# Attention and two MLPs on one core: the last block of the first MLP issued in another order, its weight splits and narrowings cut in two

## The chip, the cores and the metric

One core of a Trainium2 chip runs the whole program in one launch. The metric is the device time of one execution in microseconds (us); lower is better. A time of a kernel is the median of several executions, and the profile shows one execution of its own.

## The reference

Windowed attention with a few global keys, then two MLPs over 1536 tokens of width 512, all in float32:

```
x  = softmax(scale * q k^T + bias, masked) v      # 2 x 8 heads x 768 x 64, as 1536 x 512
h  = x @ w_in;  x = (h * cos(h)) @ w_out          # first MLP, hidden width 2048
g  = x @ w_gate; v = x @ w_val                    # second MLP, hidden width 1536
out = (g * sigmoid(g) * v) @ w_out2
```

To keep float32 accuracy, each operand of a matrix product is split into a rounded high part and a remainder, and three products are summed: high x high, high x remainder, remainder x high.

## The kernel before, in words

The tokens are three blocks of 512 (`BLOCKS`). The first MLP runs 16 hidden slices of 128 for each block, so 48 steps; a step is written s, and the last block is s = 32 to 47. The attention of the later tokens is woven into steps 0 to 31. The second MLP then runs 12 slices for each of the three blocks (`run`).

A step of the first MLP has these parts:

- `h_mm(s)`: 12 matmuls on TensorE (L278) that write one of two PSUM banks `h`. In each group of three the third is the first that needs the remainder of the weight.
- `chain_a(s)` on ScalarE (L304: rounded k = h / 2pi), `chain_f(s)` on VectorE (L315: the fraction f), `chain_sin(s)` on ScalarE (L324 sine, L325 square), then `chain_c(s)`: L331 on VectorE (the product with h), L335 on ScalarE (the high part of g), L336 (the remainder of g) on VectorE or GpSimd.
- `prep_in(s)` and `prep_out(s)` split a weight tile: a cast on ScalarE (L217, high part) and a subtraction (L218, remainder) on VectorE or GpSimd, in the last block always on VectorE. Each kind has two buffers.
- `y_mm(s)`: 12 matmuls (L349) that add slice s into four PSUM banks `y`; three matmuls for each bank, of which the third needs the remainder of the weight. It is issued two steps late: `y_mm(s-2)` follows `h_mm(s)`. At the end of a block the four banks are evicted by ScalarE (L358) and VectorE (L359), and the next block's first `y` product needs them free.

The weights come as 8-byte words. `fetch` starts a DMA into one of three staging tiles `st` (L193, queue of SyncE), and `narrow` makes float32 of them with three VectorE operations (L198, L201, L204). During the last block of the first MLP the weights of the second MLP are fetched and narrowed ahead: `ahead(u, half)`, with u = s - 32, calls `conv()`, which narrows one tile and starts the next DMA. In `run` two more are narrowed in each step, and any that is missing when a split needs it.

Up to step 31 the planner of the compiler orders each engine's instructions. `last_block()` opens a region (`manual_schedule`) in which each engine issues in exactly the order in which the code emits; engines wait for one another only through data and buffers. All that the change reorders lies in this region. Its loop before is L402 to L411:

```python
        for s in range(last, nsteps):
            chain_a(s, h_mm(s))
            prep_in(s + 1)
            chain_f(s)
            prep_out(s - 1)
            chain_sin(s)
            ahead(s - last, 0)
            chain_c(s)
            ahead(s - last, 1)
            y_mm(s - 2)
```

Of the kernel before, what the change touches and what calls it, by code (L numbers as in the profile page):

```python
# [15 lines left out]
I32 = mybir.dt.int32  # L16
AF = mybir.ActivationFunctionType
ALU = mybir.AluOpType
# [4 lines left out]
P = 128  # L23
B, H, S, D = 2, 8, 768, 64
NTOK = B * S
DM = H * D
# [44 lines left out]
LD = 5  # L71
BASES = (0, 3, 6, 8, 13, 17, 20, 23)
HN = 256
AHEAD2 = (4, 8, 12)
BLOCKS = ((0, 512), (512, 512), (1024, 512))


# [1 line left out]
def attention_moe_moe2_kernel(  # L79
# [14 lines left out]
    nc = tc.nc  # L94
    NF1 = w1i.shape[0]
# [3 lines left out]
    def f32(ap):  # L99
        return ap.bitcast(F32)  # L100
# [4 lines left out]
    ws_p = ctx.enter_context(tc.tile_pool(name="ws", bufs=2))  # L105
# [17 lines left out]
    def load_q(i):  # L123
# [16 lines left out]
        out=nval, in0=nneg, scalar=4294967296.0, in1=nf[:, :, 0], op0=ALU.mult, op1=ALU.add  # L140
# [45 lines left out]
    def fetch(src, j, pool=wr_p, tag="w"):  # L186

        if not wide:
            w = pool.tile([P, DM], F32, tag=tag, name="w")
            nc.sync.dma_start(out=w, in_=src[j])  # L190
            return lambda: w
        t = st_p.tile([P, DM, 2], I32, tag="st", name="st")
        nc.sync.dma_start(out=t, in_=src[j].bitcast(I32).rearrange("p (n w) -> p n w", w=2))  # L193

        def narrow():
            w = pool.tile([P, DM], I32, tag=tag, name="w")
            hi, lo = t[:, :, 1], t[:, :, 0]
            nc.vector.tensor_scalar(  # L198
                w, hi, 0x07FFFFFF, 3, op0=ALU.bitwise_and, op1=ALU.logical_shift_left
            )  # L200
            nc.vector.scalar_tensor_tensor(  # L201
                out=w, in0=hi, scalar=-(1 << 30), in1=w, op0=ALU.bitwise_and, op1=ALU.bitwise_or
            )
            nc.vector.scalar_tensor_tensor(  # L204
                out=w, in0=lo, scalar=29, in1=w,
                op0=ALU.logical_shift_right, op1=ALU.bitwise_or,
            )
            return w.bitcast(F32)

        return narrow  # L210

    def eng(which, n):
        return nc.vector if n < len(which) and which[n] == "D" else nc.gpsimd

    def split_w(w, tag, e=nc.gpsimd, pool=ws_p):
        s = pool.tile([P, 2, DM], F32R, tag=tag, name="ws")
        nc.scalar.copy(out=s[:, 0, :], in_=w)  # L217
        e.tensor_tensor(out=s[:, 1, :], in0=w, in1=f32(s[:, 0, :]), op=ALU.subtract)  # L218
        return s

    def x_turn(xn, ps_pool, tag):
# [12 lines left out]
    def moe(before, steps, release):  # L234

        with ExitStack() as c1:
            got = []

            def last_block(*pools):
                release()
                c1.enter_context(tc.manual_schedule())
                got.append(second_mlp(c1, *pools))
                return got[0][0]

            rest = first_mlp(c1, before, steps, last_block)
            got[0][1](rest)

    def first_mlp(c1, before, steps, last_block):  # L250
        w_in, w_out = {}, {}
        got = {}
        todo = [(b, j) for b in range(len(BLOCKS)) for j in range(NF1)]
        nsteps = len(todo)
        hp = c1.enter_context(tc.tile_pool(name="hp", bufs=2, space=PSUM))
        wis, wos, hps, hs, fs, gs, ys = {}, {}, {}, {}, {}, {}, {}
# [34 lines left out]
        def h_mm(s):  # L291
            n = BLOCKS[todo[s][0]][1]
            if s in hps:
                h_part(s, HN, n)
            else:
                hps[s] = hp.tile([P, 512], F32, tag="h", name="h")
                h_part(s, 0, n)
            wis.pop(s)
            return hps.pop(s)

        def chain_a(s, ps):
            n = BLOCKS[todo[s][0]][1]
# [23 lines left out]

        def chain_c(s):
            n = BLOCKS[todo[s][0]][1]
            h, f = hs.pop(s)[0], fs.pop(s)
            g = g_p.tile([P, 2, 512], F32R, tag="g", name="g")  # L330
            nc.vector.scalar_tensor_tensor(  # L331
                out=f[:, :n], in0=f[:, :n], scalar=0.5, in1=h[:, :n],
                op0=ALU.subtract, op1=ALU.mult,
            )
            nc.scalar.copy(out=g[:, 0, :n], in_=f[:, :n])  # L335
            eng(GLE, s).tensor_tensor(  # L336
                out=g[:, 1, :n], in0=f[:, :n], in1=f32(g[:, 0, :n]), op=ALU.subtract
            )
            gs[s] = g

        def y_mm(s):
            b, j = todo[s]
# [30 lines left out]
        ch_p = c1.enter_context(tc.tile_pool(name="ch", bufs=2))  # L373
        g_p = c1.enter_context(tc.tile_pool(name="g", bufs=2))
        yp = c1.enter_context(tc.tile_pool(name="yp", bufs=4, space=PSUM))
        last = nsteps - NF1
        for s in range(last):
            early, late = steps.get(s, ((), ()))
            if s < NF1:
                get("i", s + 2)  # L380
                get("o", s + 1)
            ps = h_mm(s)
            if s >= 2:
                y_mm(s - 2)
            prep_in(s + 1)
            if s >= 1:
                chain_b(s - 1)
            for th in early:
                th()
            if s >= 1:  # L390
                chain_c(s - 1)
            if s < NF1:
                use("i", w_in, s + 2)
                use("o", w_out, s)
            prep_out(s - 1)
            chain_a(s, ps)
            for th in late:
                th()
        ahead = last_block(ch_p, g_p, hp, yp)
        chain_b(last - 1)  # L400
        chain_c(last - 1)
        for s in range(last, nsteps):  # L402
            chain_a(s, h_mm(s))
            prep_in(s + 1)
            chain_f(s)
            prep_out(s - 1)
            chain_sin(s)
            ahead(s - last, 0)
            chain_c(s)
            ahead(s - last, 1)  # L410
            y_mm(s - 2)  # L411
        prep_out(nsteps - 1)
        return [lambda s=s: y_mm(s) for s in (nsteps - 2, nsteps - 1)]

    def second_mlp(c2, ch_p, g_p, hp, yp):


        todo = [(b, j) for b in range(len(BLOCKS)) for j in range(NF2)]
        nsteps = len(todo)
# [23 lines left out]
        def prep(nm, s):  # L443
            if s < nsteps:
                pool, tag = split_pool[nm]
                while (nm, todo[s][1]) not in w2:
                    conv()
                wsp[nm, s] = split_w(w2[nm, todo[s][1]], tag, nc.vector, pool)
# [59 lines left out]
                    nc.sync.dma_start(out=out[rows, :], in_=o)  # L508

        def ahead(u, half):  # L510
            if u == 0 and half == 0:
                get()
                get()
            if u > 0 and (half == 1 or u in AHEAD2):
                conv()
            if u == NF1 - 1 and half == 1:
                prep("g", 0)
                prep("v", 0)

        def run(rest):  # L520
            for s in range(nsteps + 1):
# [15 lines left out]
                    for _ in range(2):  # L537
                        conv()

        return ahead, run  # L540

    def windowed_path():
        m1 = const.tile([P, 3, P], F32, name="m1")
# [545 lines left out]
```

## Time and profile before

| | |
|---|---|
| time, median of 3 executions | 748.09 us (745.61 to 751.55) |
| the profiled execution | 748.84 us, span 747.0 us |
| TensorE busy | 692.3 us, 93% of the span |
| VectorE busy | 491.6 us, 66% |
| ScalarE busy | 380.0 us, 51% |
| GpSimd busy | 156.8 us, 21% |
| mean granted TensorE clock | 0.943 of full |

The span is the time from the first to the last instruction that the profile records; 1.84 us of the profiled execution lie outside it. Busy shares are means over stages that differ: the last block of the first MLP and the change to the second MLP lie between about 322 and 447 us, and only that stretch is read closely below.

### The profile page before, as it was taken

The page shows a single profiled execution, that of the slowest core. Times are in us where ns is not written, and L with a number is a line of the kernel's source. Part 1 is how long each engine was busy: PE and PEld are TensorE (multiplying, and loading weights), DVE is VectorE, ACT ScalarE, POOL GpSimd, SP SyncE. Part 2 cuts the span into 40 slices and gives each one's busy share as a digit, 9 for nine tenths or more (in the row PEclk, how much of TensorE's full clock was granted, in tenths as well). Part 3 has the DMA queues.
Part 4 walks back from the last instruction along what each step waited for, and adds up shares of the span by engine and source line. Part 5 has one row for each costly group of instructions (what it writes and reads, how often), then busy time and mean ns, then how long its engine had stood idle before and what let it go on. Part 6 is the DMA issues. An engine that isn't in the chain of part 4 may idle for free.

```text
span 747.0 us, 9145 instructions
## 1 busy us (share of the span) xinstructions
PE 692.3 (93%) x3280; PEld 532.5 (71%) x3282; DVE 491.6 (66%) x950; ACT 380.0 (51%) x770; POOL 156.8 (21%) x135
## 2 busy tenths in 40 slices
PE   8897797998999999998888789999999999999996
PEld 3355575766677778876666568888888888888884
DVE  5778999999986675438778748977344434343441
ACT  2664657566498889655544543333343333333331
POOL 2545553654545535420000000000000000000000
PEclk8856898799999999999999979999999999999999
DMA  6769746755541232002332313440010000100001
GB/s 211 163 151 229 211 129 185 172 134 171 147 123 43 57 61 41 17 1 60 110 112 85 95 46 113 141 142 28 1 57 0 1 0 1 57 0 1 1 0 61
DMA packets 69510, 62.73 MB, mean 84 GB/s; under 512 B 48881, under 2 KB 55025, under 8 KB 69457
## 3 DMA queue, kind: packets, MB, share of 16 engines
q1 hardware_dynamic: 69456, 62.08, 30.6%
q8 instruction: 27, 0.44, 0.2%
q14 instruction: 27, 0.21, 0.1%
HBM read 47.19 MB, written 3.15 MB: 67 GB/s over the span
## 4 chain that ended last, share of the span: by engine, by line
PE 64%; DVE 25%; ACT 5%; DMA 3%; issue 2%; DVEq 0%; SPq 0%; ACTq 0%
PE v L458 13%; PE g L458 13%; PE o L494 13%; PE h L278 8%; PE y L349 7%; PE s L696 6%; DVE w L201 4%; DVE w L204 4%; DVE w L198 3%; DVE f L331 2%; DVE f L315 2%; DVE ws L218 2%; DMA st<-w1i 2%; DVE g L336 2%; DVE sb L715 1%
## 5 line engine op out<-in xcount | busy, mean ns | idle before, releaser
L218 DVE TENSOR_TENSOR ws<-w,ws 128x512 fp32r<-128x512 f32 x160 | 113.1, 729 | 108.3 <-ACT ws L217 108.2
L278 PE MATMUL h<-xh,ws 128*128 128x512 f32 (+1 forms) x392 | 138.6, 415 | 17.5 <-DVE ws L218 10.1
L349 PE MATMUL y<-g,ws 128*128 128x512 f32 x576 | 141.5, 394 | 4.1 <-DVE xl L359 3.0
L349 PEld LDWEIGHTS y<-g,ws 128*128 128x128 f32 x576 | 109.0, 190 | 29.2 <-DVE xl L359 3.4
L217 ACT CAST ws<-w 128x512 fp32r<-128x512 f32 x204 | 120.2, 615 | 9.8 <-PE y L349 3.6
L278 PEld LDWEIGHTS h<-xh,ws 128*128 128x128 f32 x392 | 76.1, 199 | 44.5 <-DVE ws L218 15.5
L494 PE MATMUL o<-ws,a 128*128 128x512 f32 x432 | 104.9, 392 | 0.0
L458 PE MATMUL g<-xh,ws 128*128 128x512 f32 x288 | 96.9, 398 | 5.8 <-ACT ws L217 4.5
L458 PE MATMUL v<-xh,ws 128*128 128x512 f32 x288 | 96.3, 395 | 0.0
L494 PEld LDWEIGHTS o<-ws,a 128*128 128x128 f32 x432 | 81.0, 188 | 18.7 <-DVE a L481 0.4
L278 PE MATMUL h<-xl,ws 128*128 128x512 f32 (+1 forms) x196 | 79.6, 407 | 0.1
L470 ACT ACTIVATE sl<-g 128x512 f32<-128x512 f32 x36 | 21.5, 598 | 110.3 <-PE g L458 110.3
L218 POOL TENSOR_TENSOR ws<-w,ws 128x512 fp32r<-128x512 f32 x44 | 61.5, 1398 | 73.4 <-ACT ws L217 58.5
L696 PE MATMUL s<-kr,qr 64*128 64x256 f32 (+1 forms) x192 | 61.2, 460 | 8.2 <-DVE mx L715 4.1
L458 PEld LDWEIGHTS g<-xh,ws 128*128 128x128 f32 x288 | 55.0, 191 | 18.3 <-ACT ws L217 4.9
L458 PEld LDWEIGHTS v<-xh,ws 128*128 128x128 f32 x288 | 54.2, 188 | 12.7
L480 ACT CAST a<-sl 128x512 fp32r<-128x512 f32 x36 | 22.4, 623 | 75.0 <-DVE sl L476 75.0
L458 PE MATMUL g<-xl,ws 128*128 128x512 f32 x144 | 57.0, 396 | 0.0
L458 PE MATMUL v<-xl,ws 128*128 128x512 f32 x144 | 56.9, 395 | 0.0
L733 ACT ACTIVATE sb<-sb,nm 128x256 f32<-128x256 f32 (+1 forms) x96 | 45.9, 480 | 21.1 <-DVE nm L723 21.0
L696 PEld LDWEIGHTS s<-kr,qr 64*128 64x128 f32 x192 | 35.8, 225 | 28.5 <-DVE mx L715 8.5
L324 ACT ACTIVATE f<-f 128x512 f32<-128x512 f32 x48 | 30.3, 632 | 48.7 <-DVE f L315 48.6
(102 smaller groups left out, 884.8 us busy)
## 6 DMA issues: line engine op xcount, KB each, us to landing
st<-w1i SPq DMA_DIRECT2D x16, 512.0 KB, 3.8
st<-w1o SPq DMA_DIRECT2D x16, 512.0 KB, 4.3
st<-w2g SPq DMA_DIRECT2D x12, 512.0 KB, 3.7
st<-w2v SPq DMA_DIRECT2D x12, 512.0 KB, 3.7
st<-w2o SPq DMA_DIRECT2D x12, 512.0 KB, 3.7
vr<-v SPq DMA_DIRECT2D x16, 256.0 KB, 3.3
kr<-kT SPq DMA_DIRECT2D x12, 256.0 KB, 3.6
qr<-qT SPq DMA_DIRECT2D x12, 256.0 KB, 4.7
```

The costliest lines, as they stand in the source:

```text
L198: nc.vector.tensor_scalar(w, hi, 0x07FFFFFF, 3, op0=ALU.bitwise_and, op1=ALU.logical_shift_left)
L201: nc.vector.scalar_tensor_tensor(out=w, in0=hi, scalar=-(1 << 30), in1=w, op0=ALU.bitwise_and, op1=ALU.bitwise_or)
L204: nc.vector.scalar_tensor_tensor(out=w, in0=lo, scalar=29, in1=w, op0=ALU.logical_shift_right, op1=ALU.bitwise_or,)
L217: nc.scalar.copy(out=s[:, 0, :], in_=w)
L218: e.tensor_tensor(out=s[:, 1, :], in0=w, in1=f32(s[:, 0, :]), op=ALU.subtract)
L278: nc.tensor.matmul(hps[s][:, c0:c1], lhsT=wis[s][:, a, k * P:(k + 1) * P], rhs=xx[:, k, t0 + c0:t0 + c1], start=(k == 0 and a == 0 and xx ...
L324: nc.scalar.activation(out=f[:, :n], in_=f[:, :n], func=AF.Sin, scale=PI)
L349: nc.tensor.matmul(ys[b][m][:, :n], lhsT=w[:, a, m * P:(m + 1) * P], rhs=g[:, c, :n], start=(j == 0 and a == 0 and c == 0), stop=(j == NF1 ...
L458: nc.tensor.matmul(ps[:, :n], lhsT=w[:, a, k * P:(k + 1) * P], rhs=xx[:, k, t0:t0 + n], start=(k == 0 and a == 0 and xx is xh), stop=(k == ...
L494: nc.tensor.matmul(os_[b][m], lhsT=a[:, c, m * P:(m + 1) * P], rhs=w[:, d, :], start=(j == 0 and c == 0 and d == 0), stop=(j == NF2 - 1 an ...
L696: nc.tensor.matmul(o, lhsT=qr[r, i % 3, c, :], rhs=k, start=True, stop=True)
L733: nc.scalar.activation(out=a, in_=a, func=AF.Exp, bias=nm[:, h:h + 1], accum_out=sm[:, h:h + 1])
```

## The change

Only the last block of the first MLP, the start of the second, and the helpers that they use are rewritten.

- `split_w` is cut into `split_hi` (the cast) and `split_lo` (the remainder), and `chain_c` loses its last operation to a new `chain_d` (the remainder of g). Steps before the last block call the pairs one right after the other.
- `narrow` can be called in two pieces: a call with `half=0` issues L198 and L201 alone; the next call issues the third operation.
- In the last block the casts of the input weights are issued two steps ahead (`hi_in(s + 2)`), their remainders one step ahead, the cast of an output weight one step after its own and its remainder one step later still. `chain_c` and `chain_d` of a step are issued in the step after.
- One tile is narrowed in each of the steps u = 2 to 15, its first piece in the step before. Before, one was narrowed in each of u = 1 to 15, and one more at u = 4, 8 and 12 (`AHEAD2`).
- The splits of the second MLP's first two tiles, g0 and v0, are issued in the last two steps (`first`).

```diff
+        def narrow(half=None):
             hi, lo = t[:, :, 1], t[:, :, 0]
+            if not part:
+                w = pool.tile([P, DM], I32, tag=tag, name="w")
+                part.append(w)
+                nc.vector.tensor_scalar(
+                    w, hi, 0x07FFFFFF, 3, op0=ALU.bitwise_and, op1=ALU.logical_shift_left
+                )
+                nc.vector.scalar_tensor_tensor(
+                    out=w, in0=hi, scalar=-(1 << 30), in1=w,
+                    op0=ALU.bitwise_and, op1=ALU.bitwise_or,
+                )
+            w = part[0]
+            if half == 0:
+                return None
             nc.vector.scalar_tensor_tensor(
                 out=w, in0=lo, scalar=29, in1=w,
...
+    def split_hi(w, tag, pool=ws_p):
         s = pool.tile([P, 2, DM], F32R, tag=tag, name="ws")
         nc.scalar.copy(out=s[:, 0, :], in_=w)
+        return s
+
+    def split_lo(s, w, e):
         e.tensor_tensor(out=s[:, 1, :], in0=w, in1=f32(s[:, 0, :]), op=ALU.subtract)
...
+        def hi_in(s):
+            if s < nsteps:
+                wis[s] = split_hi(w_in[todo[s][1]], "wi")
+
+        def lo_in(s):
+            if s < nsteps:
+                split_lo(wis[s], w_in[todo[s][1]], nc.vector)
...
-        chain_b(last - 1)
-        chain_c(last - 1)
+        chain_f(last - 1)
+        chain_sin(last - 1)
+        hi_in(last + 1)
         for s in range(last, nsteps):
-            chain_a(s, h_mm(s))
-            prep_in(s + 1)
+            ps = h_mm(s)
+            chain_c(s - 1)
+            if s > last:
+                lo_out(s - 2)
+            chain_d(s - 1)
+            ahead(s - last, 1)
+            if s + 1 < nsteps:
+                lo_in(s + 1)
+            else:
+                first(1)
+            chain_a(s, ps)
             chain_f(s)
-            prep_out(s - 1)
+            hi_out(s - 1)
             chain_sin(s)
             ahead(s - last, 0)
-            chain_c(s)
-            ahead(s - last, 1)
+            if s + 2 < nsteps:
+                hi_in(s + 2)
+            elif s + 2 == nsteps:
+                first(0)
             y_mm(s - 2)
-        prep_out(nsteps - 1)
+        chain_c(nsteps - 1)
+        lo_out(nsteps - 2)
+        hi_out(nsteps - 1)
+        chain_d(nsteps - 1)
+        lo_out(nsteps - 1)
...
         def ahead(u, half):
-            if u == 0 and half == 0:
-                get()
-                get()
-            if u > 0 and (half == 1 or u in AHEAD2):
+            if half == 0:
+                if u == 0:
+                    get()
+                    get()
+                elif u < NF1 - 1 and got:
+                    got[0][1](0)
+            elif u > 1:
                 conv()
-            if u == NF1 - 1 and half == 1:
-                prep("g", 0)
-                prep("v", 0)
```

In the changed kernel `lo_in` and `lo_out` use VectorE always; so the remainder of the output weight of step 31, which GpSimd made before, is VectorE's.

## Rows read from the trace of the kernel before

**Rows 1.** Busy time by stretch: from:to, length, then each engine's busy us and count, clock.

```profile
344.57:424.33 79.76, 69.67 (x289) 52.90 (x289) 63.69 (x105) 40.42 (x71) 0.00 (x0) 1.00 0.31 99
...
431.50:438.53 7.03, 5.65 (x12) 4.01 (x13) 4.28 (x8) 2.79 (x4) 0.00 (x0) 0.50 0.25 75
...
447.33:500.00 52.67, 52.67 (x231) 43.10 (x230) 46.23 (x79) 18.92 (x36) 0.00 (x0) 1.00 0.40 123
500.00:650.00 150.00, 150.00 (x654) 122.68 (x653) 67.26 (x106) 50.92 (x92) 0.00 (x0) 1.00 0.06 22
```

**Rows 2.** TensorE in order of time: start us, us, operation, idle before and releaser.

```profile
322.11 0.39 PE L278 MATMUL h<-xh,ws 128*128 128x512 f32 x1
...
332.99 0.39 PE L278 MATMUL h<-xh,ws 128*128 128x512 f32 x1
...
338.83 3.02 PE L349 MATMUL y<-g,ws 128*128 128x512 f32 x12 [2.96 <-DVE xl L359]
...
424.17 2.88 PE L349 MATMUL y<-g,ws 128*128 128x512 f32 x12
431.50 0.80 PE L458 MATMUL g<-xh,ws 128*128 128x512 f32 x1 [4.45 <-ACT ws L217]
...
438.53 3.41 PE L349 MATMUL y<-g,ws 128*128 128x512 f32 x12
441.78 0.40 PE L458 MATMUL v<-xh,ws 128*128 128x512 f32 x1
...
447.33 0.39 PE L458 MATMUL g<-xh,ws 128*128 128x512 f32 x1
```

**Rows 3.** Waits, 330 to 430 us: total us, times, longest.

```profile
PE h L278 <- DVE ws L218: 10.1, 11, 1.4
```

**Rows 4.** VectorE in order of time, one step of the last block.

```profile
396.81 0.69 DVE L331 SCALAR_TENSOR_TENSOR f<-f,h 128x512 f32<-128x512 f32 x1 [0.77 <-ACT f L325]
398.24 0.69 DVE L336 TENSOR_TENSOR g<-f,g 128x512 fp32r<-128x512 f32 x1 [0.74 <-ACT g L335]
398.85 0.42 DVE L198 TENSOR_SCALAR w<-st 128x512 int32<-128x512 int32 x1
399.31 0.69 DVE L201 SCALAR_TENSOR_TENSOR w<-st,w 128x512 int32<-128x512 int32 x1
400.03 0.69 DVE L204 SCALAR_TENSOR_TENSOR w<-st,w 128x512 int32<-128x512 int32 x1
400.64 0.68 DVE L218 TENSOR_TENSOR ws<-w,ws 128x512 fp32r<-128x512 f32 x1
401.24 0.68 DVE L315 SCALAR_TENSOR_TENSOR f<-h,k 128x512 f32<-128x512 f32 x1
401.84 0.68 DVE L218 TENSOR_TENSOR ws<-w,ws 128x512 fp32r<-128x512 f32 x1
403.29 0.69 DVE L331 SCALAR_TENSOR_TENSOR f<-f,h 128x512 f32<-128x512 f32 x1 [0.76 <-ACT f L325]
```

**Rows 5.** ScalarE in order of time, the same step.

```profile
397.59 0.62 ACT L335 CAST g<-f 128x512 fp32r<-128x512 f32 x1 [0.81 <-DVE f L331]
...
398.61 1.13 ACT L217 CAST ws<-w 128x512 fp32r<-128x512 f32 x2
...
401.96 0.63 ACT L324 ACTIVATE f<-f 128x512 f32<-128x512 f32 x1 [2.22 <-DVE f L315]
402.62 0.63 ACT L325 ACTIVATE f<-f 128x512 f32<-128x512 f32 x1
```

**Rows 6.** ScalarE in order of time, steps 33 and 34.

```profile
330.47 0.60 ACT L304 ACTIVATE k<-h 128x512 int32<-128x512 f32 x1 [0.25 <-PE h L278]
...
335.56 2.05 ACT L358 ACTIVATE xh<-y 128x512 fp32r<-128x512 f32 x4
```

**Rows 7.** VectorE in order of time, step 34.

```profile
338.09 2.48 DVE L359 SCALAR_TENSOR_TENSOR xl<-y,xh 128x512 fp32r<-128x512 f32 x4
```

**Rows 8.** DMA issues of the page: count, KB each, median us to landing.

```profile
st<-w2g SPq DMA_DIRECT2D x12, 512.0 KB, 3.7
```

More of the change, by code (lines that the diff above doesn't have):

```diff
@@ L73 @@
 HN = 256
-AHEAD2 = (4, 8, 12)
 BLOCKS = ((0, 512), (512, 512), (1024, 512))
@@ L190, in fetch @@
             nc.sync.dma_start(out=w, in_=src[j])
-            return lambda: w
+            return lambda half=None: w
         t = st_p.tile([P, DM, 2], I32, tag="st", name="st")
         nc.sync.dma_start(out=t, in_=src[j].bitcast(I32).rearrange("p (n w) -> p n w", w=2))
-        def narrow():
-            w = pool.tile([P, DM], I32, tag=tag, name="w")
+        part = []
+        def narrow(half=None):
             hi, lo = t[:, :, 1], t[:, :, 0]
[L198 to L203, printed above, removed]
+            if not part:
[11 more added lines that the diff above has]
+                return None
             nc.vector.scalar_tensor_tensor(
@@ L213, in eng, with split_w @@
         return nc.vector if n < len(which) and which[n] == "D" else nc.gpsimd
-    def split_w(w, tag, e=nc.gpsimd, pool=ws_p):
+    def split_hi(w, tag, pool=ws_p):
         s = pool.tile([P, 2, DM], F32R, tag=tag, name="ws")
         nc.scalar.copy(out=s[:, 0, :], in_=w)
+        return s
+    def split_lo(s, w, e):
         e.tensor_tensor(out=s[:, 1, :], in0=w, in1=f32(s[:, 0, :]), op=ALU.subtract)
+    def split_w(w, tag, e=nc.gpsimd, pool=ws_p):
+        s = split_hi(w, tag, pool)
+        split_lo(s, w, e)
         return s
@@ L244, in last_block @@
                 got.append(second_mlp(c1, *pools))
-                return got[0][0]
+                return got[0][:2]
             rest = first_mlp(c1, before, steps, last_block)
-            got[0][1](rest)
+            got[0][2](rest)
     def first_mlp(c1, before, steps, last_block):
@@ L328, in chain_c @@
             n = BLOCKS[todo[s][0]][1]
-            h, f = hs.pop(s)[0], fs.pop(s)
+            h, f = hs.pop(s)[0], fs[s]
             g = g_p.tile([P, 2, 512], F32R, tag="g", name="g")
@@ L335, in chain_c, with chain_d @@
             nc.scalar.copy(out=g[:, 0, :n], in_=f[:, :n])
+            gs[s] = g
+        def chain_d(s):
+            n = BLOCKS[todo[s][0]][1]
+            g, f = gs[s], fs.pop(s)
             eng(GLE, s).tensor_tensor(
@@ L338, in chain_c @@
             )
-            gs[s] = g
         def y_mm(s):
@@ L398, in first_mlp, with hi_out, lo_out @@
                 th()
-        ahead = last_block(ch_p, g_p, hp, yp)
-        chain_b(last - 1)
-        chain_c(last - 1)
-        for s in range(last, nsteps):
-            chain_a(s, h_mm(s))
-            prep_in(s + 1)
+        ahead, first = last_block(ch_p, g_p, hp, yp)
+        def hi_in(s):
[4 more added lines that the diff above has]
+                split_lo(wis[s], w_in[todo[s][1]], nc.vector)
+        def hi_out(s):
+            wos[s] = split_hi(w_out[todo[s][1]], "wo")
+        def lo_out(s):
+            split_lo(wos[s], w_out[todo[s][1]], nc.vector)
+        chain_f(last - 1)
+        chain_sin(last - 1)
+        hi_in(last + 1)
+        for s in range(last, nsteps):
+            ps = h_mm(s)
+            chain_c(s - 1)
+            if s > last:
+                lo_out(s - 2)
+            chain_d(s - 1)
+            ahead(s - last, 1)
[4 more added lines that the diff above has]
+            chain_a(s, ps)
             chain_f(s)
-            prep_out(s - 1)
+            hi_out(s - 1)
             chain_sin(s)
             ahead(s - last, 0)
-            chain_c(s)
-            ahead(s - last, 1)
+            if s + 2 < nsteps:
+                hi_in(s + 2)
+            elif s + 2 == nsteps:
+                first(0)
             y_mm(s - 2)
-        prep_out(nsteps - 1)
+        chain_c(nsteps - 1)
[3 more added lines that the diff above has]
+        lo_out(nsteps - 1)
         return [lambda s=s: y_mm(s) for s in (nsteps - 2, nsteps - 1)]
@@ L510, in ahead, with first @@
         def ahead(u, half):
-            if u == 0 and half == 0:
-                get()
-                get()
-            if u > 0 and (half == 1 or u in AHEAD2):
-                conv()
-            if u == NF1 - 1 and half == 1:
-                prep("g", 0)
-                prep("v", 0)
+            if half == 0:
[5 more added lines that the diff above has]
+            elif u > 1:
+                conv()
+        def first(half):
+            for nm in "gv":
+                pool, tag = split_pool[nm]
+                w = w2[nm, 0]
+                if half == 0:
+                    wsp[nm, 0] = split_hi(w, tag, pool)
+                else:
+                    split_lo(wsp[nm, 0], w, nc.vector)
         def run(rest):
@@ L538, in run @@
                         conv()
-        return ahead, run
+        return ahead, first, run
     def windowed_path():
```

## Prediction, made before the run

> **What bounds the kernel now.** I read the busy time by stretch first. After 447 us TensorE is busy without a gap at full clock, up to 650 us in the rows shown; in the last block of the first MLP it is busy 69.67 of 79.76 us although its clock is full there [rows 1]. So the loss lies in that block and in the step to the second MLP, and TensorE's starts give its size [rows 2]. Where nothing holds it, two steps take 332.99 - 322.11 = 10.88 us: a dense step is 5.44 us, 2.72 for `h` and 2.72 for `y`. Measured against that pace:
>
> - the `y` product of slice 32 was due at 332.99 + 2.72 = 335.71 and starts at 338.83, 3.12 us late, held by the evictions L359;
> - from 335.71 to the `y` product of slice 45 at 424.17 are 13 steps: 88.46 us, and 13 x 5.44 = 70.72. Excess 17.74, the 3.12 included;
> - from 424.17 to the second `g` product at 447.33 are 23.16 us. Five products lie there (`y`, g0, `y`, v0, `y`). The last two take 447.33 - 441.78 = 5.55, the others need 3 x 2.72 at full clock: 13.71. Excess 9.45: 4.45 idle ahead of g0, which waits for the split of its weight, and then g0 at half clock (0.50 in 431.50 to 438.53, i.e. 1.2 GHz [rows 1]), with a further wait inside.
>
> Why a step of the block is long is told by the waits: TensorE's `h` waits 11 times for the weight remainder L218 on VectorE [rows 3]. VectorE is not short of time, it is caught in a ring. Follow one step from L331 at 396.81 to L331 at 403.29 [rows 4, 5], start to start: L331 to L335 on ScalarE 0.78; to L336 0.65; to L198 0.61; to L201 0.46; to L204 0.72; to L218 0.61; to L315 0.60; to the sine L324 0.72; to the square L325 0.66; to L331 again 0.67. Sum 6.48, just the distance of the two rows. Three operations for the narrowing and one remainder stand in the ring, while VectorE idles 0.77 ahead of L331 and 0.74 ahead of L336. A step with a second narrowing puts that one between L315 and L331 and runs over (three such steps).
>
> **The change, part by part.** The count of operations hardly changes; what changes is what stands in the ring.
>
> *The ring after.* In the new order VectorE issues L331 of step s-1, the output remainder, L336 of step s-1, L204, the input remainder, L315 of step s, L198, L201. L198 and L201 fall behind L315, into the wait for sine and square: 0.60 + 0.46 + 0.69 = 1.75 us after L315 they are done, and L331 can't start before 0.72 + 0.66 + 0.67 = 2.05. The output remainder falls between L331 and L336: 0.60 + 0.68 = 1.28 against 0.78 + 0.65 = 1.43. What is left is 0.72 + 0.66 + 0.67 + 0.78 + 0.65 + 0.61 (L336 to L204) + 0.61 (to L218) + 0.60 (to L315) = 5.30 us. That is 0.14 under the dense 5.44: TensorE paces the block. ScalarE has no new work: the cast two steps ahead starts 0.63 after the square and ends at 2.05 + 0.62 - 0.04 = 2.63 from L315, before L335 at 2.83; its buffer was left by `h_mm(s)`, which ended before L304. This cover is thin: each 0.1 us more in the ring beyond 0.14 would show as 0.1 per step.
>
> *The start of the block.* The evictions L358 and L359 now stand ahead of less. In step 33, L304 starts at 330.47 and lasts 0.60 [rows 6]; L315 at 331.10, sine 331.82, square 332.48, the early cast its 0.63 later at 333.11, the first L358 half of a cast pair's 1.13 later [rows 5], 333.65. The four L358 step by 0.48 (2.05 for four [rows 6]); the first ends at 334.25 and the four L359 step by 0.60 (2.48 for four [rows 7]), the last starting at 336.08. So the first `y` bank is free at about 334.96, before `y` of slice 32 is due at 335.71: the 3.12 us go. But a new wait is late next. That product's third matmul (0.45 in) needs the output remainder of step 32, and this now queues on VectorE behind the four L359 and L331 of step 33: L331 336.68, remainder 337.28 to 337.96. TensorE, due for it at 336.16, waits 1.8 us. The price runs from 0 (were the remainder issued ahead) to the old 3.12; I take 1.8, the sum of the rows. L315 is then 2.25 us behind the `y` start in step 35, where 0.83 is the least; the `y` product tolerates 2.56 (L315 + 2.05 + 0.60 + 0.68 against 5.44 + 0.45), and the lag shrinks by 0.14 a step. No second wait.
>
> *The step to the second MLP.* g0's and v0's casts come in step 46 and their remainders in step 47, ahead of L315 of 47: two casts hold up L335 by about 0.2 and one remainder more adds 0.60 to that ring, harmless, since `y` of slice 46 starts 5.44 us after that of 45 and `y` of 47 another 5.5 later. So g0 follows at once, without the idle 4.45 that precede the half clock. The longest idle left is the 1.8 above, and the old 2.96 in the same place was followed by matmuls at full pace (12 in 3.02 us [rows 2]). The whole 9.45 goes.
>
> *Work deferred.* 14 tiles are narrowed in the block instead of 18. Four go to `run`, at 1.79 us of VectorE each (L198 to L218 [rows 4]), and with them four DMA issues of SyncE. The present steps of `run` with two narrowings already run beside a TensorE busy 52.67 of 52.67, VectorE 46.23; later it is busy only 67.26 of 150 [rows 1]. 7.2 us fit there: nothing. By the order of use, one tile (v of slice 11) is narrowed on demand, two products (2 x 2.72) ahead of its use. A fetch lands in 3.7 us [rows 8] and is issued when the tile three earlier is narrowed, so two steps remain: nothing. GpSimd loses one remainder, VectorE gains it in step 33, in a wait.
>
> *Sum:* -17.74 + 1.80 - 9.45 = -25.4. From the profiled 748.84 (0.75 above the median shown): **723.5 us**, 3.3% below the median.
>
> **A rule that speaks against it.** The rows show VectorE operations of 0.68 or 0.69 us that start 0.60 or 0.61 apart [rows 4]: a follower starts before the other's recorded end. The Trainium skill, "VectorE: DVE Perf Modes", section "Terms" (DRAIN), says that the next operation can't issue until the pipe is empty, and its rules for kernel authors advise fewer operations rather than other waits; nearly the same number of operations would then buy little.
>
> **Rivals.**
> 1. *The ring is longer than I reckon.* If each of the three direct hand-overs in it took the full 0.69 instead of 0.60, it would be 5.30 + 0.25 = 5.55, 0.11 over TensorE: at most 12 x 0.11 = 1.3 us, 724.8. This is what the DRAIN rule would make of it; the 0.60 of the rows speaks against. 4%.
> 2. *The moved operations don't fit their gaps.* The gaps have 0.30 and 0.15 us to spare, and semaphores with more partners may cost what no row shows. The bound is the old ring, 6.48: 12 x 1.04 = 12.5, so 736; half of it (5.9 a step) gives about 729. For: covers of 0.15 are thin. Against: the same hand-overs are all in the rows. 14%, between 727 and 736.
> 3. *Nothing comes of it:* the engines take another order than the code emits, or the block's loss returns in `run`, 745 to 750. Against: the rows of VectorE stand in the order of the loop quoted, operation for operation. 5%.
> 4. *Slower than before.* Steps 0 to 31 are ordered by the planner, which sees later work too and may draw another order for the changed program, with remainders of GpSimd and VectorE worse placed. To lose over 1% it has to cost (25.4 + 7.5) / 32 = 1.03 us in each of these steps; at 1.1 the time is 759. Against: what is emitted up to step 31 is the same, in the same sequence. 3%.
>
> The forecast itself, 719 to 727, has 74%: below it lies the 1.8 that may not appear (721.7) and the 2.5 us by which the executions shown fall under their median. The range takes it and the nearer half of rival 2: **719 to 731**. About 1% is what can be told from no change; faster by more 92%, within 5%, slower 3%.
>
> **What will show it.** In the changed trace: `h` steps of 5.44 in the block, with no wait of L278 for L218; L198 and L201 between L315 and L331; a wait of about 1.8 us inside the first `y` product of the block, for L218 and not L359; g0 right behind `y` of slice 45, full clock throughout; from g1 to the end the same 299.7 us. Wrong would be steps of 5.6 or more with L335 or L331 as releaser (rivals 1, 2), a first `h` of the block that starts off 322 by several us (rival 4), or new waits of the second MLP for L204 (rival 3).

## The result and the profile after

| | before | after |
|---|---|---|
| time, median of 4 executions each | 746.85 us (742.67 to 751.55) | 723.58 us (716.90 to 729.03) |
| the profiled execution, and its span | 748.84 us, 747.0 us | 729.03 us, 726.8 us |
| first `h` product of step 34 to second `g` product | 114.34 us | 89.11 us |
| from there to the end of the span | 299.67 us | 299.40 us |

The ratio of the times is 0.9657, 95% interval 0.9554 to 0.976: faster, 723.58 us where 723.5 was forecast; how much of that closeness is luck is said below. (A ratio leaves out disturbed executions, the medians do not, so the two can differ by a few tenths of a per cent.)

In the code after, `h` is L292 (before L278), `y` L367 (L349), the cast L224 (L217), the remainder L228 (L218), the narrowing L201, L204, L211 (L198, L201, L204), k L318 (L304), L329 (L315), sine and square L338, L339 (L324, L325), L345 (L331), the cast of g L349 (L335), L355 (L336), the evictions L376 and L377 (L358, L359), g and v L509 (L458).

The third row of the table, called *the stage* from here on, is the measure for everything below: the two ends are matmuls that every kernel has, and all of the change lies between them (before: 332.99 to 447.33 [rows 2]). It leaves out that step 34 began at 338.29 us in this execution, 5.3 us later than in the one of before; over the twelve executions profiled here it began between 326.2 and 338.3, and TensorE's instructions stand in the same order before it in the two kernels.

The busy time by stretch, after: from:to, length, busy us (count) of PE, PEld, VectorE, ScalarE and GpSimd, then granted clock, share and GB/s of the DMA engines.

```profile
338.29:427.40 89.11, 87.47 (x385) 72.03 (x384) 74.75 (x123) 57.45 (x99) 0.00 (x0) 1.00 0.26 83
427.40:520.00 92.60, 92.60 (x405) 75.75 (x404) 77.11 (x128) 33.05 (x60) 0.00 (x0) 1.00 0.35 108
```

TensorE, which was busy 69.67 of 79.76 us in the block [rows 1], is busy 87.47 of 89.11 in the whole stage, and the clock is full in all of it, also where it was 0.50. Behind it nothing is lost: 92.60 of 92.60, with the four deferred narrowings inside.

VectorE in order of time, after, one step of the last block: start, duration, what, and in brackets the idle time before it with its releaser.

```profile
361.00 0.69 DVE L329 SCALAR_TENSOR_TENSOR f<-h,k 128x512 f32<-128x512 f32 x1
361.60 0.42 DVE L201 TENSOR_SCALAR w<-st 128x512 int32<-128x512 int32 x1
362.05 0.69 DVE L204 SCALAR_TENSOR_TENSOR w<-st,w 128x512 int32<-128x512 int32 x1
363.05 0.69 DVE L345 SCALAR_TENSOR_TENSOR f<-f,h 128x512 f32<-128x512 f32 x1 [0.31 <-ACT f L339]
363.66 0.68 DVE L228 TENSOR_TENSOR ws<-w,ws 128x512 fp32r<-128x512 f32 x1
364.48 0.69 DVE L355 TENSOR_TENSOR g<-f,g 128x512 fp32r<-128x512 f32 x1
365.09 0.69 DVE L211 SCALAR_TENSOR_TENSOR w<-st,w 128x512 int32<-128x512 int32 x1
365.69 0.69 DVE L228 TENSOR_TENSOR ws<-w,ws 128x512 fp32r<-128x512 f32 x1
366.30 0.68 DVE L329 SCALAR_TENSOR_TENSOR f<-h,k 128x512 f32<-128x512 f32 x1
```

From L329 to L329 are 5.30 us, the sum that was forecast, against 6.48 [rows 4, 5]. Two narrowing operations stand where VectorE waited for the square, one remainder where it waited for L349 on ScalarE; of the 0.77 idle ahead of L331 [rows 4], 0.31 is left. That is VectorE while it catches up. Once it has, TensorE is the pace: L329 follows L329 by 5.44 at 403.64 and 409.08.

### The profile page after: what moved, and what is told of

Same layout as the page of the kernel before. It is cut to its first block, busy times and chain, and to the rows that moved or that the text cites. A ratio compares the mean times of both kernels' runs of the same rounds, so it can differ in the third digit from the quotient of the medians.

```text
span 726.8 us, 9135 instructions
## 1 busy us (share of the span) xinstructions
PE 691.1 (95%) x3280; PEld 534.5 (74%) x3282; DVE 490.1 (67%) x951; ACT 381.6 (53%) x770; POOL 152.5 (21%) x134
## 4 chain that ended last, share of the span: by engine, by line
PE 77%; DVE 17%; ACT 2%; issue 1%; DMA 1%; POOL 0%; DVEq 0%; SPq 0%; ACTq 0%; POOLq 0%
PE v L509 14%; PE g L509 14%; PE o L545 13%; PE h L292 13%; PE y L367 12%; PE s L758 6%; DVE w L204 3%; DVE w L211 2%; DVE w L201 2%; PE warm_ps L177 2%; DVE sb L777 2%; PE x L835 2%; DVE f L345 1%; DVE f L329 1%; DVE ws L228 1%
## 5 line engine op out<-in xcount | busy, mean ns | idle before, releaser
L228 DVE TENSOR_TENSOR ws<-w,ws 128x512 fp32r<-128x512 f32 x161 | 113.0, 722 | 94.8 <-ACT ws L224 94.6
L292 PE MATMUL h<-xh,ws 128*128 128x512 f32 (+1 forms) x392 | 138.2, 415 | 6.8 <-DVE f L345 6.1
L367 PE MATMUL y<-g,ws 128*128 128x512 f32 x576 | 140.1, 391 | 2.8 <-DVE ws L228 2.8
L224 ACT CAST ws<-w 128x512 fp32r<-128x512 f32 x204 | 121.7, 614 | 20.6 <-DVE w L211 17.4
L367 PEld LDWEIGHTS y<-g,ws 128*128 128x128 f32 x576 | 107.6, 188 | 27.3 <-DVE ws L228 3.6
L292 PEld LDWEIGHTS h<-xh,ws 128*128 128x128 f32 x392 | 78.5, 203 | 28.7 <-DVE f L345 7.5
L509 PE MATMUL v<-xh,ws 128*128 128x512 f32 x288 | 96.3, 395 | 0.0
L509 PE MATMUL g<-xh,ws 128*128 128x512 f32 x288 | 94.7, 390 | 0.0
L545 PEld LDWEIGHTS o<-ws,a 128*128 128x128 f32 x432 | 81.1, 188 | 18.4
L292 PE MATMUL h<-xl,ws 128*128 128x512 f32 (+1 forms) x196 | 80.3, 410 | 0.0
L228 POOL TENSOR_TENSOR ws<-w,ws 128x512 fp32r<-128x512 f32 x43 | 59.1, 1376 | 76.1 <-ACT ws L224 62.4
L758 PE MATMUL s<-kr,qr 64*128 64x256 f32 (+1 forms) x192 | 63.1, 473 | 8.3 <-DVE kr L699 5.5
L509 PEld LDWEIGHTS v<-xh,ws 128*128 128x128 f32 x288 | 54.2, 188 | 12.7
L509 PEld LDWEIGHTS g<-xh,ws 128*128 128x128 f32 x288 | 54.1, 188 | 11.2
L509 PE MATMUL v<-xl,ws 128*128 128x512 f32 x144 | 56.9, 395 | 0.0
L509 PE MATMUL g<-xl,ws 128*128 128x512 f32 x144 | 56.0, 389 | 0.0
L211 DVE SCALAR_TENSOR_TENSOR w<-st,w 128x512 int32<-128x512 int32 x68 | 52.1, 774 | 0.7
```

Of the source, the lines that this page charges most:

```text
L211: nc.vector.scalar_tensor_tensor(out=w, in0=lo, scalar=29, in1=w, op0=ALU.logical_shift_right, op1=ALU.bitwise_or,)
L292: nc.tensor.matmul(hps[s][:, c0:c1], lhsT=wis[s][:, a, k * P:(k + 1) * P], rhs=xx[:, k, t0 + c0:t0 + c1], start=(k == 0 and a == 0 and xx ...
L367: nc.tensor.matmul(ys[b][m][:, :n], lhsT=w[:, a, m * P:(m + 1) * P], rhs=g[:, c, :n], start=(j == 0 and a == 0 and c == 0), stop=(j == NF1 ...
L509: nc.tensor.matmul(ps[:, :n], lhsT=w[:, a, k * P:(k + 1) * P], rhs=xx[:, k, t0:t0 + n], start=(k == 0 and a == 0 and xx is xh), stop=(k == ...
L545: nc.tensor.matmul(os_[b][m], lhsT=a[:, c, m * P:(m + 1) * P], rhs=w[:, d, :], start=(j == 0 and c == 0 and d == 0), stop=(j == NF2 - 1 an ...
L758: nc.tensor.matmul(o, lhsT=qr[r, i % 3, c, :], rhs=k, start=True, stop=True)
```

## Experiments

The stage in each kernel, in one execution, with the ratio of times to the kernel before:

| kernel | stage, us | ratio (95%) |
|---|---|---|
| before | 114.34 | |
| the change | 89.11 | 0.9657 (0.9554 to 0.976) |
| the change again | 89.11 | 0.9648 (0.9556 to 0.974) |
| the change, narrowing whole | 104.25 | 0.9849 (0.9744 to 0.9954) |
| before, narrowing in pieces | 95.94 | 0.9735 (0.9629 to 0.9841) |
| the change, g0 and v0 split late | 92.30 | 0.9741 (0.9647 to 0.9834) |
| the change, one remainder ahead of the evictions | 88.88 | 0.9644 (0.9541 to 0.9748) |
| the change, one operation more in the ring | 95.54 | 0.9777 (0.9723 to 0.9831) |
| the change, one operation more in the gap | 90.30 | 0.9658 (0.9593 to 0.9723) |
| the change, one chain ahead of the evictions | 87.84 | 0.9625 (0.9541 to 0.9708) |
| the change, eight tiles narrowed in the block | 89.09 | 0.9903 (0.9862 to 0.9943) |
| before, pieces and early g0, v0 | 88.82 | 0.9676 (0.9592 to 0.976) |

A bare stage without any wait would be 2.72 + 13 x 5.44 + 13.71 = 87.15 us, by the prediction's terms.

### 1. The narrowing kept whole

```diff
             if half == 0:
...
-                elif u < NF1 - 1 and got:
-                    got[0][1](0)
```

> The changed kernel with one thing undone: the narrowing is issued whole between the remainder of g and the remainder of the input weight; casts and remainders stay where the change puts them. Stage = from the first h matmul of step 34 to the first matmul of the second g product: 114.34 us before, 89.11 us after the change. Ring theory: 0.46 + 0.72 us come back into the ring, 6.48 a step; by the start-to-start distances the output remainder of slice 45 is done 13 us later and that of 46 again 1.9 later, so the stage is 104 us and the whole about 15 us slower than the change (738 us). Rival, that it is the casts two steps ahead and the split remainders that made the gain: 89 to 91 us and 723 to 726.

Measured: 104.25. TensorE and VectorE in order of time, one step of this kernel:

```profile
372.42 0.39 PE L292 MATMUL h<-xh,ws 128*128 128x512 f32 x1
372.64 0.39 PE L292 MATMUL h<-xl,ws 128*128 128x512 f32 x1
373.24 0.73 PE L292 MATMUL h<-xh,ws 128*128 128x512 f32 x2 [0.21 <-DVE ws L228]
...
376.50 2.57 PE L367 MATMUL y<-g,ws 128*128 128x512 f32 x10 [0.23 <-DVE ws L228]
```

```profile
368.67 0.69 DVE L345 SCALAR_TENSOR_TENSOR f<-f,h 128x512 f32<-128x512 f32 x1 [1.36 <-ACT f L339]
...
375.15 0.69 DVE L345 SCALAR_TENSOR_TENSOR f<-f,h 128x512 f32<-128x512 f32 x1 [1.36 <-ACT f L339]
```

The ring is 6.48 again, and the gap ahead of L345 is empty for 1.36 us. So the pieces, not the casts two steps ahead, hold the ring short: both kernels narrow 14 tiles in the block, and the place of two operations makes 15.1 us of difference. These rows also teach how to read a wait. The step is 1.04 over 5.44, but the recorded idle is only 0.21 + 0.23. A matmul of 0.39 is followed by the next after 0.23 where nothing holds it; so the third `h` matmul, 0.60 behind the second, is 0.37 late with 0.21 shown as idle, and the matmul pair behind it takes longer too (0.73 where an undisturbed pair takes 0.62). Lateness is read from starts against the pace. The Trainium skill, "Perfetto Trace Analysis", section "Tensor Engine Instruction (MATMUL, LD_WEIGHTS)", says that the profiler computes TensorE's ends and does not observe them. The rows here, 0.39 us long and 0.22 apart, fit that, but they do not show it.

### 2. The pieces alone, in the old order

The kernel before, with `narrow(half)` of the change and nothing else of it. One tile is narrowed in each step from u = 2 on, so the number falls from 18 to 14 here too:

```diff
-            if u > 0 and (half == 1 or u in AHEAD2):
+                elif u < NF1 - 1 and got:
+                    got[0][1](0)
+            elif u > 1:
                 conv()
```

> The kernel before with one thing done: the narrowing in two pieces (first piece after the square of a step, the third operation after the remainder of g, one tile a step, no second one at u = 4, 8, 12); splits, chain and the start of the second MLP as before. Ring theory: 0.60 + 0.46 + 0.69 and the output remainder's 0.60 no longer fit the 2.05 us behind L315, so the ring is 0.78 + 0.65 + 0.61 + 0.61 + 0.60 + 2.35 = 5.60 us; the y product of slice 32 starts 1.5 us late instead of 3.1; the step to the second MLP keeps most of its 9.45. Stage 98 to 100 us (114.34 before), time about 733. Rival, that the reordered splits carry the gain: 110 or more.

Measured: 95.94, which is better than was expected: 18.4 of the 25.2 us. Its VectorE takes 5.50 from L339 (the product with h here) at 353.14 to L339 at 358.64, not the 5.60 worked out: the hand-over from the second narrowing operation to it was 0.61, not 0.69. The 0.06 over 5.44 never reached TensorE in the 13 steps.

Not all of the 18.4 belongs to the pieces. In the kernel before, three steps held a second narrowing, which is gone here. TensorE there, behind such a step and behind a plain one:

```profile
361.59 0.73 PE L278 MATMUL h<-xh,ws 128*128 128x512 f32 x2 [1.38 <-DVE ws L218]
...
368.07 0.73 PE L278 MATMUL h<-xh,ws 128*128 128x512 f32 x2 [0.75 <-DVE ws L218]
```

The step that ends at 361.59 took 7.42 us, the one behind it 6.48; three such steps make 2.8 us. Pieces with all 18 tiles were not run.

What this kernel keeps of the old loss is the step to the second MLP. TensorE in order of time there, and its clock:

```profile
408.71 2.88 PE L357 MATMUL y<-g,ws 128*128 128x512 f32 x12
414.78 0.80 PE L466 MATMUL g<-xh,ws 128*128 128x512 f32 x1 [3.19 <-ACT ws L225]
...
417.38 1.22 PE L466 MATMUL g<-xh,ws 128*128 128x512 f32 x2 [1.38 <-DVE ws L226]
...
429.50 0.39 PE L466 MATMUL g<-xh,ws 128*128 128x512 f32 x1
```

```profile
414.78:421.22 6.44, 5.06 (x12) 3.55 (x13) 4.29 (x8) 2.79 (x4) 0.00 (x0) 0.56 0.24 81
```

From 408.71 to 429.50 are 20.79 us where 13.71 are needed: g0 waits 3.19 for its cast and another 1.38 for its remainder, and the granted clock of this stretch is 0.56, so most of it runs at the lower of the two levels.

### 3. g0 and v0 split late

```diff
             if s + 1 < nsteps:
                 lo_in(s + 1)
-            else:
-                first(1)
...
-            elif s + 2 == nsteps:
-                first(0)
...
         lo_out(nsteps - 1)
+        first(0)
+        first(1)
```

> The changed kernel, with casts and remainders of the second MLP's first two tiles issued at the very end of the last block, behind all of step 47, instead of in steps 46 and 47. Theory: g0 then waits for a cast that ends 2.5 us after g0 was due and 0.4 more for the remainder; if the clock stays full the stage is 89.1 + 3.0 = 92.1 us. If the idle time brings the half clock again, as behind the 4.45 us before, another 2 to 4 us: 94 to 96. Rival, that the whole 9.45 us of the old step hang on these splits alone: 98.5.

Measured: 92.30, with the clock full, as the first theory had it. TensorE's first g0 matmul and the stretch of g0:

```profile
415.07 0.50 PE L507 MATMUL g<-xh,ws 128*128 128x512 f32 x1 [2.49 <-ACT ws L224]
```

```profile
415.07:418.36 3.29, 3.13 (x13) 2.29 (x14) 2.04 (x4) 2.27 (x3) 0.00 (x0) 1.00 0.00 0
```

The early splits are worth 3.19 us here. In experiment 2 their absence costs 7.1 (95.94 against 88.82, experiment 9), since the first wait was 0.7 longer there, the one for the remainder 1.38 where it is 0.16 here, and the clock fell.

### 4. The output remainder ahead of the evictions

The remainder of step 32 is issued before the four evictions, so the wait in the first `y` product should go:

```diff
-            if s > last:
+            if s > last and s != last + 2:
                 lo_out(s - 2)
...
+            if s == last + 1:
+                lo_out(s - 1)
             y_mm(s - 2)
```

> The changed kernel, with the output remainder of step 32 issued in step 33, ahead of the evictions of the y banks, instead of behind them. The prediction's bound says the wait of 1.64 us inside the y product of slice 32 goes: stage 89.11 - 1.64 = 87.5. Rival: VectorE is behind by the four evictions either way, and the wait only moves to the y product of slice 33, whose remainder ends at the same time as now: that product would wait 1.5 us, stage 89.0. The total differs from the changed kernel by less than its spread in either case; the stage tells.

Measured: 88.88, a gain of 0.23. TensorE in order of time:

```profile
334.17 2.88 PE L367 MATMUL y<-g,ws 128*128 128x512 f32 x12
...
338.41 0.73 PE L292 MATMUL h<-xh,ws 128*128 128x512 f32 x2 [0.91 <-DVE ws L228]
...
341.66 2.56 PE L367 MATMUL y<-g,ws 128*128 128x512 f32 x10 [0.23 <-DVE ws L228]
```

The wait named was gone, for the 12 matmuls at 334.17 run through, and two others stood in its place: the third `h` matmul of step 35, 1.07 late (338.41 against 336.89 + 0.45), then the third `y` matmul of slice 33, 0.40 (341.66 against 340.81 + 0.45). The rival had the size right, and put all of it at that `y` product. So the cause is not which remainder is last in the queue but that VectorE comes out of the four evictions late; every remainder behind them is late with it.

### 5 and 6. One more VectorE operation, in the ring or in the gap

The same subtraction of 128x512, whose result nothing uses, in 13 steps: once between the narrowing's last piece and the input remainder, once behind the first piece, ahead of L345.

```diff
             ahead(s - last, 1)
+            if 2 <= s - last < NF1 - 1:
+                idle_op()                # 5, in the ring
...
             ahead(s - last, 0)
+            if 2 <= s - last < NF1 - 1:
+                idle_op()                # 6, in the gap
```

> The changed kernel with one VectorE operation more in each of steps 34 to 46 (a subtraction 128x512 like the remainders, its result unused), put between the third narrowing operation and the remainder of the input weight, i.e. in the ring. Ring theory: 5.30 + 0.60 = 5.90 a step, 0.46 over TensorE; the output remainder of slice 45 ends 5.7 us later, that of 46 another 0.7: stage (first h of step 34 to second g product) 89.1 + 6.4 = 95.5 us. If each direct hand-over cost the full 0.69, as the DRAIN rule has it, the ring would be 6.24 and the stage 99 to 100. If only VectorE's total counts (8 operations of 0.6 plus this one are 5.4 of 5.44), 89 us, as without it.

> The same operation, in the same steps, put behind the first piece of the narrowing, i.e. into the wait for sine and square. Ring theory: 0.60 + 0.45 + 0.61 + 0.60 = 2.26 us from L315's successor on against the 2.05 there, so the ring grows by 0.21 to 5.51, 0.07 over TensorE; over 12 steps 0.8 us, of which the buffers take half: stage 89.1 to 90.0 us. If the count of VectorE operations decides, the same as with the operation in the ring (95 or 99).

Measured: 95.54 in the ring, 90.30 in the gap. VectorE in order of time with the operation in the ring (L436):

```profile
362.51 0.68 DVE L329 SCALAR_TENSOR_TENSOR f<-h,k 128x512 f32<-128x512 f32 x1
...
366.59 0.68 DVE L211 SCALAR_TENSOR_TENSOR w<-st,w 128x512 int32<-128x512 int32 x1
367.19 0.69 DVE L436 TENSOR_TENSOR relt<-xh 128x512 f32<-128x512 f32 x1
367.79 0.69 DVE L228 TENSOR_TENSOR ws<-w,ws 128x512 fp32r<-128x512 f32 x1
368.39 0.68 DVE L329 SCALAR_TENSOR_TENSOR f<-h,k 128x512 f32<-128x512 f32 x1
```

Four operations of 0.68 to 0.69 start 0.60 apart, and the step grows to 5.88, by one hand-over. VectorE with the operation in the gap:

```profile
362.23 0.69 DVE L436 TENSOR_TENSOR relt<-xh 128x512 f32<-128x512 f32 x1
362.83 0.68 DVE L345 SCALAR_TENSOR_TENSOR f<-f,h 128x512 f32<-128x512 f32 x1
...
368.33 0.68 DVE L345 SCALAR_TENSOR_TENSOR f<-f,h 128x512 f32<-128x512 f32 x1
```

From L345 to L345 are 5.50: the operation uses up the 0.31 idle and then some 0.2 more. Both kernels issue the same number of operations; the place makes 5.2 us of difference in the stage. A theory that counts operations can't give two answers. The 90.30 is 0.3 over the range expected: the 0.06 over 5.44 reached TensorE in each of the last 12 steps (0.7 us), where experiment 2, with the same 5.50, paid nothing, and the `y` product of slice 46 lost 0.46 more. Why the one kernel hid it and the other did not was not tried.

### 7. The whole chain of one step ahead of the evictions

```diff
+            if s == last + 1:
+                chain_c(s)
+                lo_out(s - 1)
             y_mm(s - 2)
```

In step 34 they are not issued again, and narrowing begins one step later, so 13 tiles instead of 14.

> The changed kernel with L345 and L349 of step 33 and the output remainder of step 32 issued in step 33 ahead of the evictions, and the narrowing started one step later (13 tiles ahead instead of 14). Theory that VectorE's lag behind the four evictions makes the wait: about 0.2 us at the first y bank and 0.3 at the slice after remain of 1.64, stage 88.0 us. Rival, that the wait moves on again: 88.9. In the total the 1 us is within the spread.

Measured: 87.84, and no wait of TensorE is listed in the stage. The first `y` product of the block starts at 340.98, due at 338.07 + 2.72 = 340.79. VectorE at the evictions:

```profile
340.23 2.48 DVE L377 SCALAR_TENSOR_TENSOR xl<-y,xh 128x512 fp32r<-128x512 f32 x4 [0.64 <-ACT xh L376]
```

VectorE has done L345 (338.31) and the remainder (338.91) before the evictions, so the block's first `y` product finds its remainder ready. That is not free: the cast L349 now stands ahead of the evictions on ScalarE too, and VectorE's first one starts 2.16 behind the beginning of step 34, where after the change it was 1.24. L329 of that step still comes sooner, 5.76 behind its beginning against 6.82; of this 0.60 is L211, which no longer stands behind the evictions since the narrowing begins a step later. The two moves were not tried apart. The kernel beats the change by 1.27 us in the stage; in the time (ratios 0.9625 and 0.9657) that can't be told.

### 8. More narrowings deferred

```diff
-                elif u < NF1 - 1 and got:
+                elif 7 <= u < NF1 - 1 and got:
                     got[0][1](0)
-            elif u > 1:
+            elif u > 7:
                 conv()
```

The stage narrows eight tiles, where the change narrows 14 and the kernel before 18: ten are deferred instead of four.

> The changed kernel, with the narrowing ahead started at u = 8: 8 tiles ahead instead of 14, the other six later in the second MLP, one on demand in each step from slice 4 on besides the two. Theory of the prediction, that deferred narrowing is free as long as VectorE's lag fits the lead of its splits: a step of three narrowings takes VectorE 9.16 us by the rows (7.37 for two, 1.79 for one more) against 8.27 of TensorE, six or seven such steps 5.3 to 6.2 us of lag, and the lead is about 5.9; so the stretch from the second g product to the end stays at 299.4 us or grows by up to 1. Rival, that each 0.89 us shows at TensorE: 304 to 306. Stage before it 88 to 89.

Measured: the stage is the same, 89.09, but the rest took 315.97, 16.6 more than the 299.40. Both theories missed this. VectorE in order of time, one step of the second MLP:

```profile
457.95 0.68 DVE L527 TENSOR_TENSOR sl<-v,sl 128x512 f32<-128x512 f32 x1
...
464.33 0.69 DVE L228 TENSOR_TENSOR ws<-w,ws 128x512 fp32r<-128x512 f32 x1 [0.74 <-ACT ws L224]
465.33 0.69 DVE L228 TENSOR_TENSOR ws<-w,ws 128x512 fp32r<-128x512 f32 x1 [0.31 <-ACT ws L224]
...
468.50 0.69 DVE L228 TENSOR_TENSOR ws<-w,ws 128x512 fp32r<-128x512 f32 x1 [0.68 <-ACT ws L224]
469.11 0.68 DVE L527 TENSOR_TENSOR sl<-v,sl 128x512 f32<-128x512 f32 x1
```

Three tiles are narrowed in such a step and none is in hand, so a tile is split right after it was narrowed: VectorE narrows, hands over to the cast on ScalarE, and waits 0.74, 0.31 and 0.68 for it. The step is 11.16 us, where a step of TensorE is 8.27 (452.22 to 460.50 in the trace after). Of the 2.89 between them the third narrowing makes some 0.9 (7.36 + 1.79 = 9.15), the waits the rest. TensorE's `g` products follow one another by 11.16 five times (464.35 to 520.14), by 8.63 before that and by 10.09 behind it: 16.6 us over its own pace, which is the whole loss. With two narrowings a step and tiles in hand, after the change, VectorE's step is 7.36 (L527 at 458.93 and 466.29): it fits.

### 9. The pieces and the early g0 and v0, nothing else

Experiment 2, with g0 split in step 47 and v0 in its second half; no cast two steps ahead, no chain issued a step later:

```diff
             prep_in(s + 1)
+            if s == nsteps - 1:
+                ahead(s - last, 2)       # prep("g", 0)
...
+                if u == NF1 - 1:
+                    prep("v", 0)
```

> The kernel before with two things done: the narrowing in pieces (as in the run of the pieces alone, whose stage was 95.94 us), and the splits of the second MLP's first two tiles issued in step 47 (g0 ahead of L315, v0 behind the square) instead of behind the last narrowing. Casts two steps ahead, remainders a step later, the chain a step later: none of these. Theory that the two edits make the whole gain: the steps stay at 5.44, g0 follows the y product of slice 45 at once, so 95.94 less the 7.1 us of the old step to the second MLP: stage 88.9 us, that of the changed kernel (89.11), time 723 to 725. Rival, that the splits issued up to two steps ahead carry a part of their own: stage 91 or more.

Measured: 88.82, as good as the whole change. TensorE in order of time:

```profile
338.74 3.01 PE L357 MATMUL y<-g,ws 128*128 128x512 f32 x12 [1.38 <-DVE xl L367]
...
409.59 2.88 PE L357 MATMUL y<-g,ws 128*128 128x512 f32 x12
412.31 0.39 PE L468 MATMUL g<-xh,ws 128*128 128x512 f32 x1
```

g0 stands right behind `y` of slice 45, and the only wait of the stage that is listed is 1.38 for the evictions at 338.74. Two edits make the gain, with the four tiles less that come along with the first. The rest of the new order (casts two steps ahead, remainders and chain a step later), which trades this 1.38 at the evictions for the 1.64 at the remainder, adds nothing that these runs can measure.

### 10. The change again

> The changed kernel again, unaltered. Its profiled execution reached step 34 at 338.29 us, that of the kernel before at 332.99, with the same order of instructions up to there. If that is the spread of executions, step 34 starts elsewhere this time (326 to 338 in the runs so far) while the stage is again 89.1 us; if it belongs to the change, step 34 starts at 338 again.

Measured: 89.11 and a wait of 1.64 once more, with step 34 beginning at 331.31 instead of 338.29. So the late beginning in the profile after is of that execution and not of the change.

## Why the prediction was right

**The block.** Excess forecast: 17.74 gone, 1.80 new. The chain of waits of the trace after, in order of time (start, duration, what), shows the whole of it:

```profile
335.77 0.61 ACT k L318
...
336.47 0.70 DVE f L329
...
337.19 0.64 ACT f L338
...
337.86 0.63 ACT f L339
338.50 0.51 ACT ws L224
339.00 0.51 ACT xh L376
...
341.34 0.68 DVE xl L377
342.02 0.59 DVE f L345
342.61 0.61 DVE ws L228
...
343.27 2.58 PE y L367 x10
345.85 2.72 PE h L292 x12
```

Up to 343.27 it runs through ScalarE and VectorE, just by the steps reckoned: k, fraction, sine, square, one cast, the evictions, L345, the remainder. Against the forecast, shifted by the 5.30 by which the step began later, the last eviction starts at 341.34 (341.38), L345 at 341.93 in VectorE's rows (341.98), and the third matmul of `y` at 343.27 (343.26). The first matmul of that product starts at 341.01, so the third was due at 341.46 and is 1.81 late: 1.80 was forecast. (The list of waits shows it as 1.64, for the reason given in experiment 1.) From then on the chain is TensorE alone, 2.72 after 2.72. The ring was reckoned at 5.30 and measured at 5.30; rival 2, gaps that don't hold what is moved into them, had 0.30 and 0.15 to go on, and the row ahead of L345 shows 0.31 left. Experiment 5 shows what it would have cost: 0.44 a step.

**The step to the second MLP.** 9.45 were to go. TensorE in order of time, after:

```profile
413.69 2.88 PE L367 MATMUL y<-g,ws 128*128 128x512 f32 x12
416.41 0.39 PE L509 MATMUL g<-xh,ws 128*128 128x512 f32 x1
...
427.40 0.39 PE L509 MATMUL g<-xh,ws 128*128 128x512 f32 x1
```

13.71 us from 413.69 to 427.40, as reckoned, against 23.16 [rows 2]. Together the stage was forecast at 87.15 + 1.80 = 88.95 and is 89.11, a gain of 25.23 where 25.4 was forecast.

That the median came out within 0.1 us of the forecast is luck beyond that. The 25.4 was taken from one execution of 748.84, while the medians differ by 23.27 (746.85 and 723.58), and the executions of the kernel after lie between 716.90 and 729.03. What bears the forecast out is the stage.

**The rule that spoke against it.** The prediction went by rows of VectorE that start 0.60 apart against the DRAIN rule of the Trainium skill, "VectorE: DVE Perf Modes", section "Terms", taken at its word (rival 1: 5.55 a step). The rows after agree with the rows before: 0.60 or 0.61 behind operations of 0.68 to 0.69, a ring of 5.30. The Trainium skill's advice on the same page, section "Rules for kernel authors", is to cut the count of operations and not the semaphores. Experiments 5 and 6 have the same count and differ by 5.2 us, so the count alone does not set the time here; what the semaphores cost no run here shows.

**Rival 3**, loss that comes back in the second MLP, did not happen (299.40 against 299.67), and **rival 4**, another order of steps 0 to 31, neither: TensorE's instructions stand in the same order in both. The sign named for rival 4 did come up, for the first `h` of the block is at 327.41 instead of 322.11; but a sign that the same kernel gives or withholds (320.43 in experiment 10) can't tell an order from the spread of executions.

**Where the working was off.**
- The lower end of the range rested on a price of 0 for the new wait, "were the remainder issued ahead". Experiment 4 did that and won 0.23 us, not 1.8. The step that failed is the one that made a place in the queue the cause; the cause is VectorE's lateness behind four evictions. Experiment 7 removes the wait by taking L345 ahead of them as well, with one narrowing operation less behind them.
- The fill of the gap was reckoned at 0.60 + 0.46 + 0.69 = 1.75, with the full 0.69 where L345 follows directly; experiment 2 measured 0.61 there. So the gap of 2.05 has 0.1 more room than the prediction gave it.
- "Work deferred: nothing" was right for four tiles, but not by a sum that carries further: VectorE's free time in later stretches was counted, not the hand-overs inside a step. Reckoned in that way ten deferred would have been nearly free too, and they cost 16.6 us (experiment 8). Thirteen left in the block are still enough (experiment 7: 425.91 to the span's end at 725.7 is 299.8).
- The prediction priced all parts together. It did not ask which of them the gain needs; experiment 9 shows that the casts two steps ahead and the chain issued a step later are not among those. Nor did it price by itself that three steps lose their second narrowing (2.8 us, experiment 2).

## What to carry to other kernels

Where an engine is busy 80% and still the bound, walk one step from an operation to its next occurrence, start to start, over all engines; the operations met on the way are the price, and one that can be put into a wait of that walk costs nothing as long as the wait is longer than its hand-over. Before crediting a wait with what it shows, ask what its engine does next: if the engine itself is late, a reordering moves the wait to the next consumer. Before calling deferred work free, reckon the later step that takes it up in the same way: in experiment 8 the work fitted VectorE's free time on the whole, but not the step, and tiles taken up right after they were made waited at each hand-over.

## What the runs showed that had not been expected

- TensorE's clock after idle time, in one place of the program, ahead of g0: 2.49 us of idle left it at 1.00 (experiment 3); after 3.19 the next 6.44 us, with a second wait of 1.38 in them, were granted 0.56 on the mean (experiment 2), and after 4.45 the next 7.03 us 0.50 [rows 1, 2]. What sets the border between them was not tried.
- A wait of TensorE in the list is some 0.17 us shorter than the lateness it stands for (1.64 against 1.81; in experiment 1, 0.21 against 0.37), which adds up where each step has two.
